# The mean of the second token tile taken by halves on two engines, and one chunk's layer-norm sums moved from VectorE to ScalarE

## The chip, the cores and the metric

The kernel runs on one core of a Trainium2 chip. The metric is the device time of one execution, in microseconds (us); lower is better. Every run in this document was in the fast state, with a granted TensorE clock of 1.00 in the records. The engines are called by the profile's short names where lines are quoted: PE is TensorE's matmuls, PEld its weight loads, DVE VectorE, ACT ScalarE, POOL GpSimd, SPq the DMA issues of SyncE.

## The reference

The program is two transformer layers with the same weights: a dilated sliding-window attention with residual, then a gated MLP with residual, each on a layer norm without gain. Cut to what matters:

```python
def _layernorm(x, axis=-1, eps=1e-5):
    m = jnp.mean(x, axis=axis, keepdims=True)
    v = jnp.var(x, axis=axis, keepdims=True)
    return (x - m) / jnp.sqrt(v + eps)
# x: (1, 2048, 1024) bf16; wqkv: (1024, 3072); w1, w3: (1024, 3584); w2: (3584, 1024)
x = A_x
x = x + attention(_layernorm(x), A_wqkv, A_wo)   # 32 heads, window 8, dilation 2
x = x + mlp(_layernorm(x), B_w1, B_w3, B_w2)     # silu(x w1) * (x w3), then w2
x = x + attention(_layernorm(x), A_wqkv, A_wo)
x = x + mlp(_layernorm(x), B_w1, B_w3, B_w2)
```

## The kernel before

Tokens are handled in 16 tiles of 128 and 4 chunks of 512. A "Q stage" computes Q, K and V of a chunk (192 matmuls of 512 columns), a "T stage" does the attention of half a chunk on VectorE and then its output projection on TensorE (32 matmuls), and a "B stage" is the MLP of a chunk.

The layer norm of a chunk, used by the Q and B stages (cut):

```python
    def ln(c, first=False):
        ...
        def stats(j, after=()):          # two bn_stats of 512 and a bn_aggr, all on VectorE
        def root(j0, j1):                # sqrt on ScalarE, reciprocal on VectorE
        def apply(j):                    # (x - mean) * rstd on VectorE, into xn[j]
        for j in range(TPC):
            stats(j)
        root(0, TPC)
        for j in range(TPC):
            apply(j)
            dma(256, xb[:, :, j * P:(j + 1) * P], xn[j][:], [("xn", j)], ..., transpose=True)
```

The first Q stage is special. It starts with tiles 0 and 1 only centred (the division by the deviation is made up for later), transposes them on TensorE and starts multiplying while weight rows of 256 KB are still arriving. In the kernel before, tile 0's mean is taken by halves, tile 1's by ScalarE alone:

```python
        dve(0.77, ... tensor_scalar(xn[2][:, 0:512], x_sb[0][:, 0:512], 1.0 / D, 0.0, ..., accum_out=mean[:, 0:1]), ...)
        act(0.82, ... activation(xn[3][:, 0:512], x_sb[0][:, 512:1024], ACTF.Copy, scale=1.0 / D,
                                 accum_out=part[:, 0:1]), ...)
        act(1.25, ... activation(xn[3][:], x_sb[1][:], ACTF.Copy, scale=1.0 / D, accum_out=mean[:, 1:2]), ...)
        for j in range(2):
            ...                          # subtract the mean on VectorE (two halves), transpose on TensorE,
                                         # evacuate: tile 0 in pieces (0,2) DVE, (2,4) DVE, (4,8) ACT,
                                         # tile 1 in pieces (0,4) DVE, (4,8) ACT
        for j in range(2):
            act(1.25, ... ACTF.Square, bias=mean[:, j:j + 1], scale=-1.0, accum_out=part[:, j:j + 1]), ...
            ...                          # root, normalise, DMA transpose for the K and V stages
```

## Time and profile before

| quantity | value | from |
|---|---|---|
| time | 1614.94 us, median of 3 (1614.82 to 1615.42) | the timed runs |
| PE busy | 1601.3 of 1613.1 us | the page, part 1 |
| DVE and ACT busy | 1122.3 and 329.6 us | the page, part 1 |
| all waits of PE | 1.3 us (0.77, 0.16, 0.39), all before 7 us | the waits, and the timeline of PE |
| first matmul of the K stage | 21.49 us | the timeline |

PE is busy 99% of the span, so a change can only gain where PE waits or runs slowly. Here are the page's header, its line of the engines and the head of the chain that ended last, for the kernel before:

```profile
span 1613.1 us, 19082 instructions
...
PE 1601.3 (99%) x7463; PEld 762.7 (47%) x7610; DVE 1122.3 (70%) x1906; ACT 329.6 (20%) x526; POOL 5.3 (0%) x28
...
PE 99%; issue 1%; DMA 0%; ACT 0%; DVE 0%; ACTq 0%
PE bank L347 98%; PE bank L535 0%; PE bank L521 0%; DMA x<-in_A_x_dram 0%; PE bank L430 0%; ACT L281 0%; DVE xn L472 0%; ACT xn L460 0%; DVE x L700 0%; ACTq L460 0%
```

The waits of PE, as "engine, line waited for: us in total, times, longest":

```profile
PE bank L285 <- PEq L757: 0.8, 1, 0.8
PE bank L430 <- DVE xn L472: 0.4, 1, 0.4
PE bank L521 <- DMA slot<-in_A_wqkv_dram: 0.2, 1, 0.2
```

The first is the launch. The second is the target of half the change: PE waits for tile 1's subtraction. These are the lines of the timeline around it (start, duration, engine, line, operation, operands, count, and in brackets the idle time before and what ended it):

```profile
3.10 0.69 DVE L454 TENSOR_SCALAR_CACHE_REDUCE xn<-x 128x512 bf16<-128x512 bf16 x1 [2.10 <-DMA x<-in_A_x_dram]
...
4.53 0.72 PE L430 MATMUL bank<-ident,xn 128*128 128x128 bf16 x8
...
5.37 1.06 ACT L460 ACTIVATE xn<-x 128x1024 bf16<-128x1024 bf16 x1 [1.35 <-DMA x<-in_A_x_dram]
...
5.96 0.62 PE L521 MATMUL bank<-hT,slot 128*128 128x128 bf16 x8 [0.16 <-DMA slot<-in_A_wqkv_dram]
...
6.33 0.19 ACT L460 ACTIVATION_READ_ACCUMULATOR xn<-x 128x1 f32 x1
...
6.55 0.62 DVE L472 TENSOR_SCALAR xn<-x,mean 128x512 bf16<-128x512 bf16 x2 [1.22 <-ACT xn L460]
...
6.96 0.66 PE L430 MATMUL bank<-ident,xn 128*128 128x128 bf16 x8 [0.39 <-DVE xn L472]
...
21.49 2.75 PE L347 MATMUL bank<-xnT,slot 128*128 128x512 bf16 x11
```

Read it as a chain. Tile 1 has landed at 5.37, ScalarE sums it until 6.52 (1.06 us and a read-out of the accumulator of 0.19), VectorE subtracts from 6.55, and PE, which ran out of work at 6.58, starts the transposes at 6.96.

### The profile page before, as it was taken

What the parts mean: (1) busy time and instruction counts of PE and PEld (TensorE: products, weight loads), DVE (VectorE), ACT (ScalarE), POOL (GpSimd) and SP (SyncE); (2) the same over time, 40 slices, a digit from 0 to 9 for tenths busy, and PEclk for the clock granted to TensorE, in tenths of its full rate; (3) what the DMA queues carried; (4) which work ended last, traced back from release to release, by engine and by line L of the source; (5) the groups of instructions that cost most, each with busy time, mean ns of one, the idle gap of its engine ahead of it and who ended that gap; (6) DMA issues with size and microseconds to landing.
All of it is one profiled execution on the core that took longest, in us unless ns stands there. A gap on an engine that the chain in (4) does not pass through costs nothing.

```text
span 1613.1 us, 19082 instructions
## 1 busy us (share of the span) xinstructions
PE 1601.3 (99%) x7463; PEld 762.7 (47%) x7610; DVE 1122.3 (70%) x1906; ACT 329.6 (20%) x526; POOL 5.3 (0%) x28
## 2 busy tenths in 40 slices
PE   9999999999999999999999999999999999999999
PEld 7555544444444444444444444444444444444444
DVE  5899888988889888898898729884299831211211
ACT  5423322021201222113311032110321101101110
POOL 1000000000000000000000000000000000000000
PEclk9999999999999999999999999999999999999999
DMA  9834755495548764858545487365873464454451
GB/s 321 228 105 151 221 166 171 127 227 158 171 141 253 194 186 137 216 164 251 176 131 163 157 248 228 121 176 174 254 220 118 160 179 156 144 177 149 156 167 42
DMA packets 350649, 285.80 MB, mean 177 GB/s; under 512 B 72288, under 2 KB 344928, under 8 KB 350560
## 3 DMA queue, kind: packets, MB, share of 16 engines
q1 hardware_dynamic: 350128, 283.94, 58.8%
q8 instruction: 59, 0.97, 0.2%
q10 hardware_dynamic: 432, 0.66, 0.1%
q14 instruction: 30, 0.25, 0.1%
HBM read 238.94 MB, written 29.36 MB: 166 GB/s over the span
## 4 chain that ended last, share of the span: by engine, by line
PE 99%; issue 1%; DMA 0%; ACT 0%; DVE 0%; ACTq 0%
PE bank L347 98%; PE bank L535 0%; PE bank L521 0%; DMA x<-in_A_x_dram 0%; PE bank L430 0%; ACT L281 0%; DVE xn L472 0%; ACT xn L460 0%; DVE x L700 0%; ACTq L460 0%
## 5 line engine op out<-in xcount | busy, mean ns | idle before, releaser
L347 PE MATMUL bank<-xnT,slot 128*128 128x512 bf16 x4955 | 1088.7, 379 | 5.3
L347 PEld LDWEIGHTS <-slot 128*128 128x128 bf16 x5056 | 518.2, 102 | 572.9
L347 PE MATMUL bank<-slot,hT 128*128 128x512 bf16 (+2 forms) x1812 | 387.3, 372 | 1.9
L670 DVE TENSOR_TENSOR hT<-sg,bank 128x512 bf16<-128x512 bf16 x224 | 153.4, 685 | 214.4 <-PE bank L347 194.9
L265 DVE TENSOR_TENSOR scr<-scr 128x1024 bf16<-128x1024 bf16 (+3 forms) x576 | 293.4, 539 | 2.0
L347 PEld LDWEIGHTS <-hT 128*128 128x128 bf16 x1848 | 178.5, 98 | 208.7
L668 ACT ACTIVATE sg<-bank 128x512 bf16<-128x512 f32 x224 | 133.7, 597 | 660.5 <-PE bank L347 608.8
L265 DVE TENSOR_TENSOR scr<-qT,kT 128x2048 bf16<-128x2048 bf16 x128 | 154.1, 1219 | 73.3 <-DMA kT<-qkv_d 71.0
L405 ACT CAST sgt<-bank 128x512 bf16<-128x512 f32 x184 | 107.3, 585 | 315.2 <-PE bank L347 300.3
L265 DVE TENSOR_TENSOR scr<-pA,vT 128x2048 bf16<-128x2048 bf16 x128 | 152.5, 1220 | 0.3
L700 DVE TENSOR_TENSOR x<-x,bank 128x512 bf16<-128x512 bf16 (+1 forms) x66 | 43.9, 670 | 121.5 <-PE bank L347 121.4
L347 PE MATMUL bank<-wo,oT 128*128 128x512 bf16 x502 | 112.6, 379 | 0.6
L313 DVE BATCH_NORM_STATS2 st<-x 128x6 f32<-128x512 bf16 x124 | 81.8, 681 | 11.9 <-DMA x<-in_A_x_dram 11.4
L347 PEld LDWEIGHTS <-oT 128*128 128x128 bf16 x512 | 50.1, 98 | 60.3
L645 DVE TENSOR_TENSOR x<-x,bank 128x512 bf16<-128x512 bf16 x64 | 43.9, 687 | 37.0 <-PE bank L347 35.8
L320 ACT ACTIVATE sd<-mv,epst 128x4 f32<-128x4 f32 (+1 forms) x17 | 5.1, 297 | 172.4 <-DVE mv L316 172.1
L628 DVE STREAM_TRANSPOSE pA<-pB 128x2048 bf16<-128x2048 bf16 x16 | 37.0, 2310 | 0.5
L605 DVE STREAM_TRANSPOSE pB<-pA 128x2048 bf16<-128x2048 bf16 x16 | 37.0, 2310 | 0.5
L668 ACT ACT_TABLE_LOAD x20 | 25.7, 1283 | 56.2 <-PE bank L347 56.0
L265 DVE TENSOR_TENSOR pA<-scr 128x256 bf16<-128x256 bf16 x128 | 35.9, 286 | 0.4
L265 DVE TENSOR_TENSOR oT<-scr 128x256 bf16<-128x256 bf16 x128 | 33.9, 288 | 0.1
L327 DVE TENSOR_SCALAR xn<-x,mv,rstd 128x1024 bf16<-128x1024 bf16 x62 | 30.7, 541 | 3.5 <-DMA xnT<-xn 3.4
(61 smaller groups left out, 209.0 us busy)
## 6 DMA issues: line engine op xcount, KB each, us to landing
slot<-in_B_w_dram SPq DMA_DIRECT2D x160, 1024.0 KB, 5.9
slot<-in_A_wqkv_dram SPq DMA_DIRECT2D x28, 1024.0 KB, 5.1
qkv_d<-sgt SPq DMA_DIRECT2D x92, 256.0 KB, 3.3
qT<-qkv_d SPq DMA_DIRECT2D x16, 512.0 KB, 5.7
slot<-in_B_w_dram SPq DMA_DIRECT2D x16, 512.0 KB, 5.7
kT<-qkv_d SPq DMA_DIRECT2D x14, 544.0 KB, 6.7
vT<-qkv_d SPq DMA_DIRECT2D x14, 544.0 KB, 4.9
out_dram<-x SPq DMA_DIRECT2D x31, 128.0 KB, 4.3
```

The lines of the kernel that those rows point to most:

```text
L265: return lambda _: nc.vector.tensor_tensor(o, a, b, op=op)
L313: dve(0.67, lambda _, hh=hh: nc.vector.bn_stats(st[q][:, j, hh, :], x_sb[n][:, hh * 512:(hh + 1) * 512]), [("x", n, hh)] + list(after), [( ...
L320: act(0.3, lambda _: nc.scalar.activation(sd[q][:, j0:j1], mv[q][:, j0:j1, 1], ACTF.Sqrt, bias=epst[:]), [("mv", q, j) for j in range(j0, ...
L327: dve(0.5, lambda _: nc.vector.tensor_scalar(xn[j][:], x_sb[n][:], mv[q][:, j, 0:1], rstd[q][:, j:j + 1], op0=ALU.subtract, op1=ALU.mult), ...
L347: nc.tensor.matmul(bank[a.bank][:, 0:ncol], lhsT=w, rhs=r, start=first and i == 0, stop=last and i == n - 1)
L405: evac(act, 0.59, lambda _, a=a, i=i, m=m: nc.scalar.copy(sgt[i][:, m % 2, :], bank[a.bank][:]), op, [], [("sgt", i, m % 2)], a)
L605: dve(2.31, lambda _: nc.vector.transpose(psmT[:].rearrange("p c d -> p (c d)"), psm[:].rearrange("p w s -> p (w s)")), allA, ["pB"])
L628: dve(2.31, lambda _: nc.vector.transpose(At[:].rearrange("p w s -> p (w s)"), AeT[:].rearrange("p c d -> p (c d)")), ["pB"], allA)
L645: evac(dve, t1(512), lambda _, xs=xs, a=a: nc.vector.tensor_tensor(xs, xs, bank[a.bank][:], op=ALU.add), op, [("x", n, hh)], [("x", n, hh) ...
L668: evac(act, 0.6, lambda _, i=i, a=ag: nc.scalar.activation(sg[i][:], bank[a.bank][:], ACTF.Silu), og, [], [("sg", i)], ag, table="silu")
L670: evac(dve, t1(512), lambda _, i=i, a=au, f=f: nc.vector.tensor_tensor(hT[:, f, :], sg[i][:], bank[a.bank][:], op=ALU.mult), ou, [("sg", i ...
L700: evac(dve, t1(cn), lambda _, xs=xs, a=a, cn=cn: nc.vector.tensor_tensor(xs, xs, bank[a.bank][:, 0:cn], op=ALU.add), op, [("x", n, hh)], [ ...
```

## The change

Half 1: tile 1 is averaged like tile 0, half on VectorE and half on ScalarE, and evacuated in three pieces like tile 0. Its sum of squares on ScalarE also moves, behind tile 3's evacuation. Half 2: for the last chunk of the first Q stages (chunk 3, layer 0), mean and variance come from two ScalarE passes with an accumulator instead of `bn_stats` on VectorE. The core of the diff:

```diff
+        def sums(j):
+            act(1.25, ... activation(xn[j][:], xt[:], ACTF.Copy, scale=1.0 / D, accum_out=mv[q][:, j, 0:1]), ...)
+            act(1.35, ... activation(xn[j][:], xt[:], ACTF.Square, bias=mv[q][:, j, 0:1], scale=-1.0,
+                                     accum_out=mv[q][:, j, 1:2]), ...)
...
         for j in range(TPC):
-            stats(j)
-        root(0, TPC)
+            if on_act:
+                sums(j)
+            else:
+                stats(j)
+        root(0, TPC, D if on_act else 1)
...
-        b = ln(c)
+        b = ln(c, on_act=l == 0 and c == NCH - 1)
...
-        act(1.25, ... activation(xn[3][:], x_sb[1][:], ACTF.Copy, scale=1.0 / D, accum_out=mean[:, 1:2]), ...)
         for j in range(2):
+            dve(0.77, ... tensor_scalar(xn[2][:, 0:512], x_sb[j][:, 0:512], 1.0 / D, 0.0, ..., accum_out=mean[:, j:j + 1]),
+                [("x", j, 0)] + [("ce", 0, 2)] * j, ...)
+            act(0.82, ... activation(xn[3][:, 0:512], x_sb[j][:, 512:1024], ACTF.Copy, ..., accum_out=part[:, j:j + 1]), ...)
...
-                       ((0, 2, "DVE"), (2, 4, "DVE"), (4, 8, "ACT")) if j == 0 else ((0, 4, "DVE"), (4, 8, "ACT")))
+                       ((0, 2, "DVE"), (2, 4, "DVE"), (4, 8, "ACT")))
...
-                [("x", j, 0), ("x", j, 1), ("mean", j)] + [("ce", 1, KT - 1)],
+                [("x", j, 0), ("x", j, 1), ("mean", j), ("xnT", b, 3, 1) if j else ("ce", 1, KT - 1)],
```

The scratch output of `sums` is `xn[j]`, the buffer that holds the previous chunk's normalised rows until their DMA transpose has read them.

More of the change, by code (lines that the diff above doesn't have):

```diff
@@ L302, with ln @@
     stage_no = [0]
-    def ln(c, first=False):
+    def ln(c, first=False, on_act=False):
         s = stage_no[0]
@@ L317, in stats, with root @@
                 [("st", q, j, 0), ("st", q, j, 1)], [("mv", q, j)], pri)
-        def root(j0, j1):
-            act(0.3, lambda _: nc.scalar.activation(sd[q][:, j0:j1], mv[q][:, j0:j1, 1], ACTF.Sqrt, bias=epst[:]),
+        def sums(j):
+            xt = x_sb[c * TPC + j]
+            keys = [("x", c * TPC + j, hh) for hh in range(2)]
+            act(1.25, lambda _: nc.scalar.activation(xn[j][:], xt[:], ACTF.Copy, scale=1.0 / D,
+                                                     accum_out=mv[q][:, j, 0:1]), keys, [("xn", j), ("mv", q, j)], 1)
+            act(1.35, lambda _: nc.scalar.activation(xn[j][:], xt[:], ACTF.Square, bias=mv[q][:, j, 0:1], scale=-1.0,
+                                                     accum_out=mv[q][:, j, 1:2]), keys, [("xn", j), ("mv", q, j)], 1)
+        def root(j0, j1, n=1):
+            act(0.3, lambda _: nc.scalar.activation(sd[q][:, j0:j1], mv[q][:, j0:j1, 1], ACTF.Sqrt, bias=epst[:],
+                                                    scale=1.0 / n),
                 [("mv", q, j) for j in range(j0, j1)] + ["eps"], [("sd", q, j) for j in range(j0, j1)], -9 if first else 0, table="sqrt")
@@ L453, in q_first @@
         ce = hT[:, 8:16, :]
-        dve(0.77, lambda _: nc.vector.tensor_scalar(xn[2][:, 0:512], x_sb[0][:, 0:512], 1.0 / D, 0.0, op0=ALU.mult,
-                                                    op1=ALU.add, accum_out=mean[:, 0:1]),
-            [("x", 0, 0)], [("xn", 2), ("mean", 0)], -9)
-        act(0.82, lambda _: nc.scalar.activation(xn[3][:, 0:512], x_sb[0][:, 512:1024], ACTF.Copy, scale=1.0 / D,
-                                                 accum_out=part[:, 0:1]), [("x", 0, 1)], [("xn", 3), ("part", 0)], -9)
@@ L459, in q_first @@
-        rows[2](6, queue="AQ", after=[("part", 0)])
-        act(1.25, lambda _: nc.scalar.activation(xn[3][:], x_sb[1][:], ACTF.Copy, scale=1.0 / D,
-                                                 accum_out=mean[:, 1:2]), [("x", 1, 0), ("x", 1, 1)],
-            [("xn", 3), ("mean", 1)], -9)
-        for j in range(2):
-            for h in range(2):
-                c0 = 512 * h
-                if j == 0:
-                    dve(0.31, lambda _, c0=c0: nc.vector.tensor_scalar(
-                        xn[0][:, c0:c0 + 512], x_sb[0][:, c0:c0 + 512], mean[:, 0:1], part[:, 0:1], op0=ALU.subtract,
-                        op1=ALU.subtract), [("x", 0, 0), ("x", 0, 1), ("mean", 0), ("part", 0)],
-                        [("xn", 0), ("xn", 0, h)], -9)
-                else:
-                    dve(0.31, lambda _, c0=c0: nc.vector.tensor_scalar(
-                        xn[1][:, c0:c0 + 512], x_sb[1][:, c0:c0 + 512], mean[:, 1:2], None, op0=ALU.subtract),
-                        [("x", 1, 0), ("x", 1, 1), ("mean", 1)], [("xn", 1), ("xn", 1, h)], -9)
+        for j in range(2):
+            dve(0.77, lambda _, j=j: nc.vector.tensor_scalar(xn[2][:, 0:512], x_sb[j][:, 0:512], 1.0 / D, 0.0,
+                                                             op0=ALU.mult, op1=ALU.add, accum_out=mean[:, j:j + 1]),
+                [("x", j, 0)] + [("ce", 0, 2)] * j, [("xn", 2), ("mean", j)], -9)
+            act(0.82, lambda _, j=j: nc.scalar.activation(xn[3][:, 0:512], x_sb[j][:, 512:1024], ACTF.Copy,
+                                                          scale=1.0 / D, accum_out=part[:, j:j + 1]),
+                [("x", j, 1)], [("xn", 3), ("part", j)], -9)
+            if j == 0:
+                rows[2](6, queue="AQ", after=[("part", 0)])
+            for h in range(2):
+                dve(0.31, lambda _, j=j, c0=512 * h: nc.vector.tensor_scalar(
+                    xn[j][:, c0:c0 + 512], x_sb[j][:, c0:c0 + 512], mean[:, j:j + 1], part[:, j:j + 1],
+                    op0=ALU.subtract, op1=ALU.subtract), [("x", j, 0), ("x", j, 1), ("mean", j), ("part", j)],
+                    [("xn", j), ("xn", j, h)], -9)
@@ L475, in q_first @@
             transposed(xn[j], [("xn", j, h) for h in range(2)], ce[:, :, j * P:(j + 1) * P],
                        [("ce", j, k) for k in range(KT)],
-                       ((0, 2, "DVE"), (2, 4, "DVE"), (4, 8, "ACT")) if j == 0 else ((0, 4, "DVE"), (4, 8, "ACT")))
-        dve(0.16, lambda _: nc.vector.tensor_tensor(mean[:, 0:1], mean[:, 0:1], part[:, 0:1], op=ALU.add),
-            [("mean", 0), ("part", 0), ("ce", 1, 0)], [("mean", 0)], -9)
+                       ((0, 2, "DVE"), (2, 4, "DVE"), (4, 8, "ACT")))
@@ L480, in q_first @@
+        dve(0.16, lambda _: nc.vector.tensor_tensor(mean[:], mean[:], part[:], op=ALU.add),
+            [("mean", j) for j in range(2)] + [("part", j) for j in range(2)] + [("ce", 1, 0)],
+            [("mean", j) for j in range(2)], -9)
         for j in range(2, TPC):
```

## The prediction

> **What bounds the kernel now.** TensorE (PE). The page gives a span of 1613.1 us, PE busy 1601.3 us (99%), granted clock 9 in every slice, and a chain of waits that is 98% one matmul helper line. After the first 22 us that chain is an unbroken row of 10.74 us pieces, 0.05 us apart. The waits of PE total 1.4 us, all in the start-up: 0.8 before the warm-up, 0.16-0.2 for a weight row, 0.39 for the subtraction of tile 1. DVE is 93-100% busy from 50 to 100 us, but PE stays 99.5% busy there.
>
> **Start-up chain, from the timeline.** Tile 1 of x lands at about 5.35. ACT averages it 5.37-6.52 (1.06 + 0.19 read-out). DVE subtracts from 6.55; PE, done with weight row 1 at 6.58, idles until 6.96; then come 8 transposes, 64 matmuls, the transposes of tiles 2 and 3 (12.74), and PE never stops again.
>
> **Half 1.** Halves on DVE and ACT side by side: 0.69 + 0.08 and 0.63 + 0.19, as tile 0 shows (3.30 to 4.02), so ready at 6.1 instead of 6.52. The subtraction with two scalars costs 0.41 per half against 0.35. First transpose possible near 6.6 instead of 6.96. I expect tile 0's third weight row (lands near 6.6, from the issue list) to go ahead of the transposes and fill that hole. [...] PE gets ahead by 0.25-0.4 us. Later margins are thin: row 5 lands near 10.6, needed near 10.65; tile 3's normalised rows are ready at 12.86, needed near 12.9. Part of the 0.35 can be eaten.
>
> The square sum of tile 1 moves from 9.28 to after tile 3's evacuation (about 14.2), so its DMA transpose is issued near 16.6 rather than 14.87. Today it takes 5.0 us, behind 2 MB of weights that drain at about 16.4; elsewhere the fastest take 3.1. I expect landing near 19.9, as today; the K stage needs it near 21.2. If ACT does its four casts first, landing is about 22 and PE stalls up to 1 us.
>
> **Half 2.** Chunk 3's statistics leave DVE (8 x 0.67 + 4 x 0.20 = about 6.2 us near 42-49) and cost ACT about 4 x (1.25 + 1.33) = 10.3 us. They write the normalised tiles as scratch, so they wait for chunk 2's DMA transposes (issued 49.3-55.9): I expect them at 53-75 us. Chunk 3's Q stage starts near 132 us, so there is slack[...]. The first attention may start up to 6 us earlier on DVE, worth nothing to PE. A root after the first Exp (74 us) would reload tables (1.28 us each in the trace), off the chain.
>
> **Sum.** About -0.3 us of 1614.94: 1614.6 us, 80% range 1613.7 to 1615.7. Chances: faster by over 2% 0.002, within 2% 0.996, slower by over 2% 0.002.
>
> **Right if:** PE's wait for tile 1's subtraction falls from 0.39 to under 0.1; the K stage's first matmul moves from 21.5 to about 21.2 and all later PE work by the same; DVE total falls about 5.5 us, ACT total rises about 10. **Wrong if:** PE waits for xnT or a weight row before 22 us (gain eaten, or up to 1 us lost), or ACT standing in front of chunk 2's transposes holds up evacuations until all 8 banks fill (a few us lost), seen as PE waits near 50-75 us.

The 0.63 us of half 1 is the trace's (0.629). The sum, -0.3 us, is the estimate: 0.25 to 0.4 us of PE's progress from half 1, part of which "can be eaten", and nothing from half 2. The 8 banks named under "wrong if" are the kernel's own (its list `bank`).

## More of the kernel before

The kernel does not write its instructions in source order. Every operation is entered with an estimated duration, and a small list scheduler plays the whole program through and sorts all operations by the start it computed. What each engine then gets is a *fixed order*, decided at build time from estimates. The T stage's projections sit in a lane of their own, so they are slotted between the groups of 8 matmuls of whatever stage runs when the estimates say that their input is ready:

```python
            for e in engines:
                if e == "PE":
                    cands = []
                    for k, ops in lanes.items():
                        if heads[k] < len(ops) and waiting[ops[heads[k]]] == 0:
                            cands.append(ops[heads[k]])
                    times = [(max(free[e], ready_at[o], bank_time(o)), -o.lane, o.seq, o) for o in cands]
                    ...                                   # the earliest start is taken
    with tc.manual_schedule():
        for op in pr.place():
            op.emit(op)
```

## The result, and the profile after

The changed kernel is correct and takes the same time: 1615.12 us (median of 6, 1614.62 to 1615.33) against 1614.99 (median of 6). The ratio is 1.0000, 95% interval 0.9987 to 1.0013. A ratio is the mean time of one kernel's fast runs over that of the other's of the same rounds, so it is not quite the ratio of the medians quoted beside it.

The interval of the ratio is about 2 us wide each way, far wider than what is at stake, so what follows uses means with the plain scatter of the runs, and the traces. All executions of the unaltered kernels give 1615.07 (38 runs, standard error 0.03) before and 1615.15 (16 runs, 0.06) after: a difference of +0.08, standard error 0.06 (in the three side-by-side comparisons +0.02, +0.04 and +0.25). The predicted -0.3 us is excluded.

The page's header, engine line and chain of the kernel after:

```profile
span 1613.4 us, 19079 instructions
...
PE 1601.9 (99%) x7463; PEld 763.1 (47%) x7610; DVE 1117.2 (69%) x1897; ACT 336.6 (21%) x541; POOL 5.0 (0%) x28
...
PE 99%; issue 0%; DVE 0%
PE bank L359 98%; PE bank L527 0%; PE bank L541 0%; PE bank L285 0%; PE bank L442 0%; DVE hT L447 0%; DVE x L706 0%
```

Its waits of PE:

```profile
PE bank L285 <- PEq L763: 0.8, 1, 0.8
```

Its timeline over the same places:

```profile
3.51 0.69 DVE L467 TENSOR_SCALAR_CACHE_REDUCE xn<-x 128x512 bf16<-128x512 bf16 x1 [2.51 <-DMA x<-in_A_x_dram]
...
4.99 0.97 PE L442 MATMUL bank<-ident,xn 128*128 128x128 bf16 x8
5.09 0.63 ACT L470 ACTIVATE xn<-x 128x512 bf16<-128x512 bf16 x1 [0.68 <-DMA x<-in_A_x_dram]
5.45 0.51 DVE L447 COPY hT<-bank 128x256 bf16<-128x256 bf16 x2 [0.26 <-PE bank L442]
...
5.80 1.62 PE L527 MATMUL bank<-hT,slot 128*128 128x128 bf16 x24
5.87 0.68 DVE L467 TENSOR_SCALAR_CACHE_REDUCE xn<-x 128x512 bf16<-128x512 bf16 x1
...
6.47 0.08 DVE L467 DVE_READ_ACCUMULATOR xn<-x 128x1 f32 x1
6.66 0.73 DVE L476 TENSOR_SCALAR xn<-x,mean,part 128x512 bf16<-128x512 bf16 x2
...
7.25 0.61 PE L442 MATMUL bank<-ident,xn 128*128 128x128 bf16 x8
...
21.71 2.54 PE L359 MATMUL bank<-xnT,slot 128*128 128x512 bf16 x10
```

The wait for tile 1 is gone, and yet the K stage starts at 21.71, not at 21.2: 0.22 us later than before. Two things are to be seen. First, the subtraction of tile 1 starts at 6.66, later than the 6.55 of before, although tile 1 had landed at 5.09: VectorE was still evacuating tile 0 (from 5.45, 0.51 us) and began its half only at 5.87. Second, PE began its first transposes at 4.99 instead of 4.53, and the eight took 0.97 us instead of 0.72. From 22 us on the traces run in parallel, 0.2 to 0.3 us apart.

Half 2 did what its costing said. The sums lie on ScalarE from 54.10 on, behind chunk 2's DMA transposes (groups of ScalarE between 40 and 80 us of the kernel after: line, operation, operands, count, then busy us, mean ns, idle us before):

```profile
L324 ACT ACTIVATE xn<-x,mv 128x1024 bf16<-128x1024 bf16 x4 | 4.6, 1160 | 0.0
L322 ACT ACTIVATE xn<-x 128x1024 bf16<-128x1024 bf16 x4 | 4.3, 1074 | 2.2 <-DMA xnT<-xn 2.2
...
L322 ACT ACTIVATION_READ_ACCUMULATOR xn<-x 128x1 f32 x4 | 0.8, 204 | 0.0
L324 ACT ACTIVATION_READ_ACCUMULATOR xn<-x,mv 128x1 f32 x4 | 0.8, 200 | 0.0
```

That is 10.5 us (4.6 + 4.3 + 0.8 + 0.8). DVE's total fell by 5.1 us; ACT's rose by only 7.0, because it also reloads its function table once less (45 loads instead of 46, 1.28 us each), tile 1's average on it is shorter (0.63 us instead of 1.06), and neighbouring instructions overlap by about 0.1 us in the records (54.10 + 1.06 is 55.16, the read-out starts at 55.07). The root comes at 67.29, before the first exponential at 77.34.

So the books are: one wait of 0.39 us removed, 5 us of VectorE work removed, nothing gained. The questions are where the start-up gain went, and whether half 2 is really worth nothing, as predicted.

### The profile page after: what moved, and what is told of

It reads as the page before. It is cut to its first block, busy times and chain, and to the rows that moved or that the text cites. A ratio compares the mean times of both kernels' runs of the same rounds, so it can differ in the third digit from the quotient of the medians.

```text
span 1613.4 us, 19079 instructions
## 1 busy us (share of the span) xinstructions
PE 1601.9 (99%) x7463; PEld 763.1 (47%) x7610; DVE 1117.2 (69%) x1897; ACT 336.6 (21%) x541; POOL 5.0 (0%) x28
## 4 chain that ended last, share of the span: by engine, by line
PE 99%; issue 0%; DVE 0%
PE bank L359 98%; PE bank L527 0%; PE bank L541 0%; PE bank L285 0%; PE bank L442 0%; DVE hT L447 0%; DVE x L706 0%
## 5 line engine op out<-in xcount | busy, mean ns | idle before, releaser
L313 DVE BATCH_NORM_STATS2 st<-x 128x6 f32<-128x512 bf16 x116 | 77.0, 682 | 10.1 <-DMA x<-in_A_x_dram 9.7
```

The source lines that it names most:

```text
L313: dve(0.67, lambda _, hh=hh: nc.vector.bn_stats(st[q][:, j, hh, :], x_sb[n][:, hh * 512:(hh + 1) * 512]), [("x", n, hh)] + list(after), [( ...
```

## The experiments

Twelve kernels ran. The time differences below are means of five runs against the mean of the kernel before of the same rounds (nine runs); with the scatter seen they are good to about 0.1 to 0.2 us.

### 1. The changed kernel again

No edit.

> The changed kernel, unaltered, run again for a finer comparison. Theory G (a gain of about 0.2 us exists but is hidden by the scatter of about 0.7 us between runs, which comes from when the first tile of x lands): mean of its runs 0.1 to 0.35 us under the mean of the kernel before; in the trace the time from TensorE's first transpose of tile 0 to the first matmul of the K stage is about 16.7 us (before: 21.49 - 4.53 = 16.96), whatever the landing time. Theory D (the gain is really eaten: by the landing of weight row 5, or by tile 3's statistics): mean within 0.1 us of the kernel before, and in the trace TensorE waits for a weight row or for tile 3 between 8 and 14 us. Theory L (half 2 costs what half 1 gains, later on): the K stage starts earlier but the span does not shrink.

Measured: 1615.24 us median, +0.04 against before. The first transposes start at 4.99 and the K stage at 21.80, 16.81 us apart, against 16.96 in the first trace of the kernel before. PE has no listed wait after the launch. The part that does not depend on when the first tile comes is a little shorter; the start as a whole is not. Theory G's lower mean did not come, nor theory D's wait between 8 and 14 us, nor theory L's earlier K stage.

### 2. Half 1 alone

```diff
-        b = ln(c, on_act=l == 0 and c == NCH - 1)
+        b = ln(c)
```

> Only the halved averaging of tile 1, its three evacuations and the later square sum; chunk 3's statistics stay on VectorE. Theories G and D: the same time as the whole change to within 0.1 us (half 2 is worth nothing). Theory L: 0.2 to 0.3 us faster than the whole change. VectorE's total returns to about 1122 us and ScalarE's to about 327 us.

Measured: 1616.05 us, +0.90. Every theory missed this. The waits of PE have a new entry, near 188 us (the waits, and the timeline of PE around it):

```profile
PE bank L359 <- DVE scr L265: 0.8, 1, 0.8
```

```profile
168.68 7.07 PE L359 MATMUL bank<-wo,oT 128*128 128x512 bf16 x31
175.58 12.25 PE L359 MATMUL bank<-xnT,slot 128*128 128x512 bf16 x55
188.62 11.60 PE L359 MATMUL bank<-xnT,slot 128*128 128x512 bf16 x52 [0.78 <-DVE scr L265]
```

The same stretch of the kernel before, and of the kernel after, shows no gap:

```profile
166.53 7.07 PE L347 MATMUL bank<-wo,oT 128*128 128x512 bf16 x31
173.44 26.93 PE L347 MATMUL bank<-xnT,slot 128*128 128x512 bf16 x122
```

```profile
166.75 7.07 PE L359 MATMUL bank<-wo,oT 128*128 128x512 bf16 x31
173.66 26.71 PE L359 MATMUL bank<-xnT,slot 128*128 128x512 bf16 x121
```

The lines with `wo,oT` are the output projection of the second attention half. After it, PE still has matmuls of chunk 3's Q stage, and then the first B stage begins. That B stage multiplies the layer norm of the very rows which the projection completes: residual addition, statistics, root, normalisation and DMA transpose lie between. The wait table names a VectorE instruction, but the DMA fits to the tenth: the four transposes of that layer norm are issued from 180.63 us on, each issue taking 1.3 us, the last at 185.36; it lands at 188.48 by the trace, and PE resumes at 188.62. In experiments 5 and 10 the profile names the DMA itself, and in all four traces with this wait (also experiment 11) PE resumes 0.14 us after that landing.

So half 2 is worth 0.9 us *if half 1 is there*, and the "0 us" of the prediction does not hold. Why is the next question.

### 3. Half 2 alone

The edit is the diff's `sums`, `root` and `q_stage` parts in the kernel before.

> Only chunk 3's sums on ScalarE; tile 1 as before. Theories G and D: within 0.1 us of the kernel before, TensorE waits 0.4 us for tile 1's subtraction as before and nowhere after 22 us. Theory L: 0.2 to 0.3 us slower than the kernel before.

Measured: 1615.37 us, +0.28 (standard error about 0.13). PE waits 0.54 us for tile 1's subtraction and 0.40 for a weight row, and nowhere after 22 us. The K stage starts at 22.02 with a start-up that is instruction for instruction that of the kernel before (21.49): in this trace tile 1 was seen at 5.89 instead of 5.37. So what it lost in this trace it lost before half 2 begins. Theory L of the expectations falls: half 2 costs nothing later on.

### 4. Tile 1's mean made later

```diff
+        act(1.25, ... activation(xn[3][:], x_sb[1][:], ACTF.Copy, scale=1.0 / D, accum_out=mean[:, 1:2]), ...)   # a second time
```

> The kernel before with tile 1's averaging on ScalarE done twice in a row, so that its mean comes about 1.1 us later. If tile 1's mean is on the critical path with no slack behind it, as both the prediction and theory G have it: 0.8 to 1.1 us slower than before and TensorE's wait for the subtraction 1.4 to 1.5 us instead of 0.39. Theory D says that part of a delay is absorbed too: 0.2 to 0.7 us slower, because what comes next waits for data anyway.

Measured: 1616.32 us, +1.14. PE waits 1.20 us for the subtraction and 0.25 for the evacuation after it; the K stage starts at 22.89. A later mean is paid in full. That looks like proof of a critical path, but it only tells one direction; experiment 7 tells the other.

### 5. Half 1 with chunk 3's normalisation later

In half 1 alone VectorE's fixed order has chunk 3's four normalisations in the middle of the first attention's scores, and there it stood four times until chunk 2's DMA transposes had left the buffers (timeline of VectorE, half 1 alone):

```profile
54.38 0.55 DVE L336 TENSOR_SCALAR xn<-x,mv,rstd 128x1024 bf16<-128x1024 bf16 x1 [0.35 <-DMA xnT<-xn]
55.68 0.55 DVE L336 TENSOR_SCALAR xn<-x,mv,rstd 128x1024 bf16<-128x1024 bf16 x1 [0.75 <-DMA xnT<-xn]
57.05 0.55 DVE L336 TENSOR_SCALAR xn<-x,mv,rstd 128x1024 bf16<-128x1024 bf16 x1 [0.83 <-DMA xnT<-xn]
58.29 0.55 DVE L336 TENSOR_SCALAR xn<-x,mv,rstd 128x1024 bf16<-128x1024 bf16 x1 [0.69 <-DMA xnT<-xn]
```

That is 2.6 us of standing, in which VectorE ran nothing of what came after in its order: with the four moved back, as in this experiment, its first output comes 3.4 us earlier (86.7 against 90.1 us), so other work was ready behind them. With half 2 the four come later by themselves. The edit moves them without half 2:

```diff
-                [("x", n, 0), ("x", n, 1), ("mv", q, j), ("rstd", q, j)], [("xn", j)] + ...
+                [("x", n, 0), ("x", n, 1), ("mv", q, j), ("rstd", q, j)] + [("oT", 0, 0)] * (s == NCH - 1), [("xn", j)] + ...
```

> Half 1 alone, with one more dependency: the four normalisations of chunk 3 come after the first attention's first output instead of in the middle of its scores; VectorE's amount of work is unchanged. Theory O (half 1 alone is 0.9 us slower because VectorE, in order, stands four times before a normalisation whose buffer chunk 2's DMA transpose has not yet left, 2.6 us in all, and so finishes the first projection's input after TensorE wants it): those waits fall from 3.9 us to about 1.3, the 0.8 us wait of TensorE near 188 us vanishes, and the time is 1615.2, as before and as the whole change. Rival W (the 6 us of statistics work on VectorE is what counts, wherever it stands): the wait near 188 us stays at 0.5 to 0.8 us, and the time is 1615.7 to 1616.1.

Measured: 1617.09 us, +2.10. The VectorE waits on transposes fell from 3.9 to 1.3 us, exactly as meant, and the first half's first output came at 86.7 instead of 90.1 us. The time got worse, and PE's wait grew (timeline of PE):

```profile
168.73 7.07 PE L359 MATMUL bank<-wo,oT 128*128 128x512 bf16 x31
...
189.63 10.74 PE L359 MATMUL bank<-xnT,slot 128*128 128x512 bf16 x48 [1.74 <-DMA xnT<-xn]
```

Theory O is dead. VectorE was not what came late: the last outputs of the second attention half started at 162.77 instead of 164.46 us, and PE took them no earlier (168.73 against 168.68 us). Rival W predicted 0.5 to 0.8 us of wait and is off as well. What stayed the same is the *place* of the projection in PE's fixed order. Counting in the instruction order how many of the 192 matmuls of chunk 3's Q stage come before the projection of the second attention half:

| kernel | Q matmuls before the projection | PE's wait near 188 us |
|---|---|---|
| before | 128 | none |
| half 2 alone | 120 | none |
| after (both halves) | 128 | none |
| half 1 alone | 136 | 0.78 us |
| half 1 with later normalisation | 136 | 1.74 us |
| half 1 with early square sum (6) | 120 | none |

The place moves in groups of 8 matmuls, 1.73 us each. Half 1 moves it one group later, half 2 one group earlier, both together not at all. This is theory P, which experiments 9 to 11 test. (The first attention half's projection moves too: it starts 82.9 us after the K stage before, 84.6 after and 86.3 in half 1 alone. No wait follows it in any of them.)

### 6. Half 1 with the square sum at its old place

```diff
-                [..., ("mean", j), ("xnT", b, 3, 1) if j else ("ce", 1, KT - 1)],
+                [..., ("mean", j), ("ce", 1, KT - 1)],
```

> Half 1 alone, with tile 1's sum of squares back at its old place, before tile 2's root. If the moved square sum is what upset the order (it delays tile 1's DMA transpose[...] by 2.4 us): no wait of TensorE near 188 us, 1615.0 to 1615.3. If the order was upset by the rest of half 1: a wait stays, 1615.6 to 1616.1. [...]

Measured: 1615.80 us, +0.68. There is no wait near 188 us (place 120), as the first alternative said, but the time is not the 1615.0 to 1615.3 that went with it. PE now waits in the start-up: 0.52 us for a weight row and 0.41 us, at 15.54, for tile 3's evacuation, because the order of tile 3's transposes and the last weight row changed. The moved square sum buys PE a start without that second wait and pays with a later place of the projection. (The delay of 2.4 us that the expectation speaks of is that of the issue of tile 1's DMA transpose: 17.29 us in the trace after against 14.87 before. The next load of SyncE's queue is issued only 0.64 us later, at 18.64 against 18.00, since the issue itself took 3.07 us before and 1.30 after.)

### 7. The bound: tile 1 needs no mean of its own

```diff
-                    xn[j][:, c0:c0 + 512], x_sb[j][:, c0:c0 + 512], mean[:, j:j + 1], part[:, j:j + 1],
+                    xn[j][:, c0:c0 + 512], x_sb[j][:, c0:c0 + 512], mean[:, 0:1], part[:, 0:1],
```

Tile 1's two half sums are dropped too, and its estimated subtraction time is lengthened so that PE's order stays that of the changed kernel. The result is wrong.

> The whole change, but tile 1 is centred with tile 0's mean, so it waits for no average of its own; wrong result on purpose. It is the upper bound of what half 1 can give. If tile 1's average still held TensorE back in the changed kernel: 0.3 to 0.6 us faster than it. If what holds TensorE back is now its own work[...], and the weight rows: within 0.15 us of the changed kernel (1615.0 to 1615.3).

Measured: 1615.11 us, +0.03 against before and within 0.1 us of the changed kernel; relative error 0.034. PE's order and that of the DMA issues are the changed kernel's in the trace. Tile 1's subtraction is done at 6.26 us, and yet PE starts its transposes only at 7.35, because the third weight row comes first and its weight loads wait for it (timelines of PEld and PE):

```profile
6.88 0.45 PEld L527 LDWEIGHTS <-slot 128*128 128x128 bf16 x8 [0.24 <-DMA slot<-in_A_wqkv_dram]
7.35 0.61 PE L442 MATMUL bank<-ident,xn 128*128 128x128 bf16 x8
```

A mean that costs nothing is worth nothing. So, in this order of PE, no way of averaging tile 1 faster could have gained the predicted 0.3 us.

### 8. The kernel before again

No edit.

> The kernel before, unaltered, for its scatter: theory C (chance) expects that the landing of x's first tile (3.10 us in the first trace) and the moment at which TensorE's weight loads drop from 0.15 to 0.10 us (4.0 us) may be found late here too (3.5 and 7 us); if they belong to half 1, they are early here: 2.9 to 3.1 and 3.6 to 4.5 us. The mean of its runs is within 0.15 us of the other runs of the same kernel.

Measured: 1615.11 us, -0.04. The trace is instructive: no wait of PE is listed between the launch and the end, and the K stage starts at 21.39 (lines of PE's timeline):

```profile
4.78 0.72 PE L430 MATMUL bank<-ident,xn 128*128 128x128 bf16 x8
5.45 1.34 PE L521 MATMUL bank<-hT,slot 128*128 128x128 bf16 x16
6.80 0.66 PE L430 MATMUL bank<-ident,xn 128*128 128x128 bf16 x8
...
21.39 2.97 PE L347 MATMUL bank<-xnT,slot 128*128 128x512 bf16 x12
```

In this run the transposes of tile 1 start at 6.80 with no listed wait before them. (The table leaves out gaps under 0.15 us. The 16 matmuls before them took 1.34 us, against 1.05 in experiment 10, because the weight loads of the second row waited 0.29 us for it.) The 0.39 us of the first trace was one throw of the dice: the four traces with the old mean (the first, this one, and experiments 3 and 10) have 0.39, 0, 0.54 and 0 us at that place. Theory C's question stays open here: the first tile was seen at 3.26 us and the weight loads still took 0.15 us at 4.14 and 0.10 from 4.77 on, between its early and its late values (0.10 from 4.03 in the first trace of the kernel before, from 5.74 in that of the kernel after).

### 9. Half 1 with the projection one group earlier

The scheduler is told 10% shorter times for the tree sums of that attention half. The instructions are the same; only their order changes.

```diff
+        ease[0] = 0.9 if (l, half) == (0, 1) else 1.0
-        dve(tt(1024), vtt(bf[:, 0:4, :], bf[:, 0:4, :], bf[:, 4:8, :], ALU.add), [k], [k])
+        dve(ease[0] * tt(1024), vtt(bf[:, 0:4, :], bf[:, 0:4, :], bf[:, 4:8, :], ALU.add), [k], [k])
```

> Half 1 alone, where the kernel's own placing of instructions is told 10% shorter times for the tree sums of the second attention half (the instructions themselves are the same), so that TensorE's fixed order has that half's output projection 8 matmuls (1.73 us) earlier: after 128 of the 192 Q matmuls of chunk 3, as in the kernel before and in the changed one, instead of after 136. Theory P (half 1 alone is slower because of this place: 56 matmuls, 12.1 us, are left to cover the way from the projection to the next stage's transposed input, which takes 13.0 to 14.0 us): the wait near 188 us is gone and the time is 1615.1 to 1615.3, 0.8 us under half 1 alone. Rival W (VectorE's statistics work counts, not the place): a wait of over 0.5 us stays, 1615.7 to 1616.1.

Measured: 1615.39 us median (1614.54 to 1615.61), mean 1615.15, +0.17. The wait is gone:

```profile
166.99 7.07 PE L359 MATMUL bank<-wo,oT 128*128 128x512 bf16 x31
173.90 26.28 PE L359 MATMUL bank<-xnT,slot 128*128 128x512 bf16 x119
```

By the means 0.7 us are back (+0.17 against +0.90) without touching half 2 and with VectorE's work unchanged. Rival W falls. The runs scatter more than any others, and the trace has two small losses that the wait table leaves out, near 36.3 us for a weight block and near 49.6 for a DMA transpose, 0.6 us in all. Why they came here is open.

### 10. The kernel before with the projection one group later

```diff
+        ease[0] = 1.05 if (l, half) == (0, 1) else 1.0
```

> The kernel before, where the placing is told 5% longer times for the same tree sums, so that the projection comes after 136 of the 192 matmuls instead of 128. Neither half of the change is in it. Theory P: the next stage's input lands 1.73 us later, at about 188.6 us, and TensorE, ready at about 187.4, waits 0.8 to 1.7 us near 188 us; 1615.9 to 1616.8. Any theory in which half 1 or VectorE's work is the cause: no such wait, 1615.1.

Measured: 1615.91 us, +0.94. Neither half of the change is in this kernel, and it has the same loss at the same place:

```profile
168.48 7.07 PE L347 MATMUL bank<-wo,oT 128*128 128x512 bf16 x31
175.39 12.25 PE L347 MATMUL bank<-xnT,slot 128*128 128x512 bf16 x55
188.54 11.82 PE L347 MATMUL bank<-xnT,slot 128*128 128x512 bf16 x53 [0.90 <-DMA xnT<-xn]
```

### 11. The changed kernel with the projection one group later

The same edit in the changed kernel.

> The changed kernel with the same longer times, projection after 136. In the changed kernel the last transposed input lands about 1.3 us before TensorE wants it. Theory P: a wait of 0.2 to 0.6 us near 188 us, less than in the kernel before because of the larger margin; 1615.3 to 1615.7. If half 2's relief of VectorE is worth more than one place: no wait, 1615.1 to 1615.3.

Measured: 1616.60 us, +1.68; PE waits 1.40 us near 188 us. Theory P was right that a wait appears and wrong about its size: I had expected 0.2 to 0.6 us from the margin of the changed kernel. The last transpose landed about 2.7 us later (188.87 against 186.18), not 1.73: after the move VectorE's order around the residual additions differs too (the normalisation starts at 180.24 instead of 178.13), and the second transpose is issued only at 182.78. A margin read from one order does not carry over to another.

With the place at 136, four kernels give the same picture. From the end of the projection (the start of the next matmul) until PE resumes, 56 matmuls cover 12.25 us:

| kernel | end of projection | PE resumes | way | less 12.25 | wait in the profile |
|---|---|---|---|---|---|
| half 1 alone | 175.58 | 188.62 | 13.04 | 0.79 | 0.78 |
| half 1, later normalisation | 175.64 | 189.63 | 13.99 | 1.74 | 1.74 |
| before, later projection | 175.39 | 188.54 | 13.15 | 0.90 | 0.90 |
| after, later projection | 175.35 | 189.01 | 13.66 | 1.41 | 1.40 |

The last two columns must agree, since the wait is what the cover leaves; what the table shows is a way longer than the cover. With the place at 128 there are 1.73 us more of cover, and no wait. The edit of experiments 9 to 11 also reorders VectorE around the residual additions, which is a rival. The landing times part the two: from the end of the projection to the landing of the last transpose it takes 13.47, 12.52 and 12.79 us with the place at 128 (before, after, experiment 9) and 12.90 to 13.85 with 136. The ways overlap; the cover is what differs. In the kernel before the last transpose is issued at 183.72 and lands at 186.91, some 0.5 us before PE gets there, an estimate from that landing and the length of 64 matmuls. The kernel was one scheduling step from losing a microsecond, and nothing in its profile showed it as a wait.

### 12. The changed kernel a third time

No edit.

> The changed kernel unaltered, a third time, to narrow the comparison and to have one more trace of the start-up. If the start-up gain is really nil on average, as the bound with no average for tile 1 says: mean within 0.1 us of the kernel before of the same rounds. First tile of x seen by VectorE at 3.25 to 3.55 us, as in the six traces of kernels with half 1, against 2.95 to 3.3 in the four without.

Measured: 1615.18 us, +0.25 of the means, the largest of the three comparisons; the expected "within 0.1 us" was missed in this one, and the pooled means above stand at +0.08. PE waits 0.21 us for a weight row in the start-up. The first tile was seen at 3.29 us, as expected.

### The start-up over all traces

Seven traces have the new start-up in PE's new order (three of the changed kernel, and experiments 2, 5, 9 and 11), four have the old one (two of the kernel before, and experiments 3 and 10).

| | old start-up, 4 traces | new start-up, 7 traces |
|---|---|---|
| first tile seen by VectorE | 3.05 to 3.53 us | 3.26 to 3.53 us |
| first transposes on PE | 4.53 to 4.92, mean 4.69 | 4.70 to 4.99, mean 4.93 |
| from there to the K stage | 16.61 to 17.48, mean 16.96 | 16.38 to 17.26, mean 16.81 |
| first matmul of the K stage | 21.39 to 22.02, mean 21.65 | 21.37 to 21.96, mean 21.74 |
| PE's listed waits for weight rows (4 to 22 us) | 0.16, 0, 0.40, 0.16 | 0, 0, 0.21, 0, 0.84, 0, 0.39 |
| third weight row lands | 6.56 to 7.01, mean 6.82 | 6.55 to 7.22, mean 6.90 |
| PE begins to load it | 7.18 to 7.93, after tile 1's transposes | 6.63 to 7.26, before them |

The way from the first transposes to the K stage became 0.15 us shorter, about half of what was predicted, and that difference is smaller than the range of either column. The first transposes started 0.24 us later. But the sum of these two parts hides what sets the K stage now: the third weight row, which the new order puts in front of tile 1's transposes. In five of the seven traces, and in experiment 7, PE's first weight load of that row begins 0.04 to 0.05 us after the row has landed (0.08 in experiment 9; in experiment 2 PE itself was 0.3 us late). From that load to the K stage it takes 14.70 to 14.78 us in all of these but the first trace after (14.92, with a further wait for a row). So an earlier mean cannot help; no run moved this row alone, so its part is read from the traces and from experiment 7.

Whether the later first transposes are chance or belong to the change is open. All instructions up to there are the same in both kernels, and experiment 10 (old start-up) saw its first tile at 3.53 us, as late as any; but the new start-up has no trace under 3.26 us. PE's speed at that time scatters as well: the eight transposes of tile 0 took 0.62 to 0.72 us in six of the eleven traces and 0.82 to 1.06 in the other five, all five with the new start-up. PE is slower at first, and not for the same time in every trace: in the first trace of the kernel before, the warm-up's matmuls of 512 columns (L285) start 0.43 us apart up to 3.71 us, against 0.216 later (29.69 to 30.99 us), and the weight loads, 0.15 us each up to 3.71, take 0.10 us from 4.03 on. In the first trace of the kernel after, loads of 0.15 us are seen up to 5.63 and loads of 0.10 us from 5.74 on. In experiment 1 the 24 matmuls of tile 0 took 1.89 us without a listed wait, against 1.05 us for 16 of them in experiment 5. What sets that moment was not shown; the granted clock reads 1.00 in these first microseconds too (both kernels, 0 to 8 us). The weight loads part this change of speed from the landing of the first tile: those of the first transposes, which wait for tile 0's subtraction, begin at 4.69 us on average in the old start-up and at 4.83 in the new. So 0.14 of the 0.24 us is a later input, and 0.10 is PE still at its warm-up (in five of the seven new traces the transposes stand behind it until 4.99).

From the K stage on the traces agree. From its first matmul to the end of PE's last one it takes 1588.83 us in nine of the 14 traces, both kernels, half 2 alone and the bound among them. It takes 1589.77 to 1590.74 in the four with the wait near 188 us (0.16 to 0.17 us more than the listed wait in each), and 1589.42 in experiment 9. So neither half gains or costs anything after the start-up, except through the place of the projection.

## Why the prediction was right or wrong

The time was inside the range (1613.7 to 1615.7), and "within 2%" was right. The forecast gain of 0.3 us did not exist. That the time stayed inside the range was luck: half 1 alone, in which the prediction saw the whole gain, lies outside it at 1616.05, and half 2, which it held to be worth nothing, brought the time back. Point by point:

1. **"What bounds the kernel now": right.** PE stays at 99%, its waits lie in the start-up, and the traces run in parallel after 22 us.
2. **"PE's wait for tile 1's subtraction falls from 0.39 to under 0.1": right as an observation**, 0.39 to 0 in the changed kernel's traces, **and worth nothing.** Experiment 7 takes the mean away altogether and gains 0.0 us; experiment 8 shows the kernel before without any wait there.
3. **"So ready at 6.1 instead of 6.52": the first step that failed.** In the trace after, tile 1 landed at 5.09, and the mean was ready at 6.55. The estimate took VectorE as free when tile 1 lands. It evacuates tile 0 at that time (the edit makes tile 1's half wait for it, `("ce", 0, 2)`), and its half began at 5.87 (at 5.85 to 5.87 in five of the seven traces). In the other two, with earlier first transposes, the mean was ready at 6.11 and 6.29, and PE then waited for the weight row of the next point.
4. **"Tile 0's third weight row (lands near 6.6) to go ahead of the transposes and fill that hole": the order was right, the landing was not, and this is the step on which the gain hung.** 6.6 is the first trace's landing (6.56), the earliest of the four with the old start-up. In the seven new traces the row landed at 6.90 on average, 0.3 us later than forecast, and the K stage followed it. It made PE wait 0.21, 0.39 and 0.84 us in three of the seven, which is the prediction's own "wrong if"; in the others PE reached it at about the time of its landing or was late itself. A wait for a mean was exchanged for a wait for weights.
5. **"PE gets ahead by 0.25-0.4 us": wrong.** From the first transposes on it gains 0.15 us, the difference of the two means; at the K stage it is not ahead (21.74 against 21.65 us).
6. **The later DMA transpose of tile 1: right.** Issued near 17.3 us (forecast 16.6), landing 3.3 us later near 20.6 (forecast 19.9), before the K stage at 21.7. The square sum ran before the casts, as hoped.
7. **The sums on ScalarE at 53 to 75 us, about 10.3 us: right** (54.10 to 67, 10.5 us). The forecast rise of ACT's total by about 10 was too high (7.0), since one table load went away, tile 1's average got shorter and the new instructions overlap; DVE's fall of 5.1 was near the 5.5.
8. **"The first attention may start up to 6 us earlier on DVE, worth nothing to PE": wrong.** The attention's time decides where the scheduler puts the projection, and the place decides whether the next stage's input is there in time. Half 1 alone costs 0.90 us through that place, and half 2 puts it back. The prediction treated PE's order as given and looked for waits in it. The list of what could go wrong (evacuations held up, weight rows) did not contain a change of that order.

That the place is the cause was shown from both sides: taking it back in half 1 alone removed the loss (experiment 9), and moving it in the kernel before, with neither half of the change, produced it (experiment 10). Open remain why the first transposes of the new start-up came later and the +0.28 us of half 2 alone, whose trace places it before half 2 begins.

No version beat both kernels. The changed kernel has no listed wait of PE left after the launch except a weight row now and then, and no experiment tried to bring that row earlier.

## What to carry to other kernels

When a schedule is computed from estimates, a small local change can move a far-away instruction by a whole group, so after such a change compare the order of instructions, not only the durations, and test each half of a two-part change alone: a null result may be two effects that cancel. Before counting a wait as gain, look at several traces of the unchanged kernel and run the bound, with the waited-for work removed altogether; and ask what PE's order puts next, here a weight row that landed just then; a slow-down that is paid in full (experiment 4) does not show that a speed-up will be paid at all (experiment 7). A stage that does not wait may still have only half a microsecond to spare; measure the margin at each hand-over before moving work near it.

## Durations that the traces showed

- ScalarE: one copying ACTIVATE of 128 x 1024 bf16 with an accumulator took 1057 to 1094 ns in the traces of both kernels, one of 128 x 512 took 629 to 630. The read-out of the accumulator is a separate instruction of 186 to 222 ns; at 512 elements (0.63 and 0.19 us) that is nearly a quarter of the total.
- DMA transposes: one of 128 x 1024 bf16 from SBUF to SBUF kept the issuing queue for 1.3 us (median of the 62 in the kernel before) and landed 3.1 us after its issue at the fastest, 3.4 us in the median and 7.2 us at the slowest. In the start-up, with the DMA engines 80% busy or more until 16.7 us, the first took 5.6 us before and 5.9 us after. The kernel's own estimate (0.45 us for the issue) is far below.
